# Attention scores taken from float32 q and k directly, in place of rounded halves and remainders

## The chip, the cores and the metric

The kernel runs on one core of a Trainium2 chip. The metric is the device time of one execution in microseconds; the kernel before is given by the median of 3 runs.

## What is computed

Attention with a threshold, 8 batches of 8 heads, 576 queries and keys, 64 columns a head, and behind it an RWKV feed-forward (FFN) on the attention's output. All inputs and the output are float32.

```python
scores = scale * np.matmul(q, k.transpose(0, 1, 3, 2))          # 8 x 8 x 576 x 576
thresh = np.max(scores, axis=-1, keepdims=True) - tau
scores = np.where(scores >= thresh, scores, -1000000000.0)
attn = np.exp(scores - np.max(scores, axis=-1, keepdims=True))
attn = attn / (np.sum(attn, axis=-1, keepdims=True) + 1e-09)
x = np.matmul(attn, v)                       # heads side by side: 8 x 576 x 512
xk = mu_k * x + (1.0 - mu_k) * x_prev        # x_prev: the row before
xr = mu_r * x + (1.0 - mu_r) * x_prev
k = np.maximum(xk @ w_k, 0.0)                # 512 -> 1024
out = sigmoid(xr @ w_r) * (k * k @ w_v)      # 1024 -> 512
```

## The kernel before

The attention goes by jobs: one job is one batch and two heads (32 pairs; batch 0 is cut into two halves, so there are 36 jobs). The two heads' q and k lie transposed in one tile `raw`: 64 rows for each head, 1216 columns (576 of q, 64 last keys, 576 keys). ACT scales the q part by 1/8. A job works in units:

- a P unit is 128 queries of both heads. Its scores fill two PSUM buffers named `s`, one for each head (`s_0`, `s_1`), of 128 x 576 float32 each. There are only these two. There are 128 P units.
- a T unit is the last 64 queries of both heads, in one buffer `s`. There are 32 T units.

For each head of a unit, DVE takes the row maximum (L555), ACT the threshold (L563) and the exponential (L571) from PSUM to `p`, DVE the mask and the row sum (L579), which is the last reader of `s`. DVE inverts the sums (L589, L590), POOL multiplies `p` by them (L604), PE transposes `p` in blocks of 128 (L628) into buffers `w`, ACT and DVE copy them to `pm` and `pl` (L646, L648). Each 256 or 320 queries of a job are one attend (L708): float32 matmuls with 64 weight columns, one head in each half of the array's columns. The result goes to `xT`. Behind each batch stand FFN chunks of 256 rows: L853 for w_k, L895 for w_r, L917 for w_v. The FFN's matmuls take float32r operands, each value as a rounded part and a remainder, three products for each matmul.

The scores use the same idea. ACT rounds `raw` to `hi` (L434), POOL makes the remainder `lo` (L440), and DMAs of the SP queue copy both into `st` tiles of 128 rows: `st1` has hi above lo, `st2` has lo above hi. With 128 rows of contraction, `st1` and `st2` as weights against `st1` as the moving operand give all four products of halves (L521), 4 matmuls of 288 columns for each head. T units use block-diagonal weights `bd` (four ACT copies, L484) and three products (L496). Only the first job (`PLAIN = 1`) takes its scores straight from `raw` in float32 (L510).

Order: every step is given to a planner with an engine, an estimated time and a key; the planner places steps in the order in which they could start, by its own estimates of time and of free buffers. The order of each engine's instructions is then fixed, and an engine goes through its list in order. Scores, transposes and attends have keys far ahead of the FFN's, which fills what is left of PE. In the profile PEld is PE's weight load.

Of the kernel before, what the change touches and what calls it, by code (L numbers as in the profile page):

```python
# [8 lines left out]
F32 = mybir.dt.float32  # L9
FR = mybir.dt.float32r  # L10
AF = mybir.ActivationFunctionType
ALU = mybir.AluOpType
# [205 lines left out]
def tile_threshold_attention_then_rwkv_ffn(  # L218
# [12 lines left out]
    V, A, G, PE, SY = nc.vector, nc.scalar, nc.gpsimd, nc.tensor, nc.sync  # L231
# [3 lines left out]
    P = 128  # L235
    B, NPAIR, _, _ = qk.shape
    D = P // 2
    S = out.shape[1]
# [4 lines left out]
    SM = 512  # L243
    ST = S - SM
    HS = S // 2
    KT = S
    W = 2 * S + ST
# [11 lines left out]
    add = plan.add  # L259
    DQ = 0.55  # L260
    HALF = 1
    W0, W1, W2, W3, AVK = 3.0, 3.5, 50.0, 2.0, 4.5
    PREP, PB, VB, COLD, EARLY = 8, 2, 2, 24, 30
# [3 lines left out]
    def sbuf(tag, shape, dtype=F32, bufs=1):  # L267
        return plan.buf(sb, tag, shape, dtype, bufs)
# [4 lines left out]
    def fixed(name, shape, dtype=F32):  # L273
        return plan.buf(const, name, shape, dtype, make=lambda: const.tile(shape, dtype, name=name))
# [12 lines left out]
        writes=[(small, 0)],  # L287
        key=-100,
# [5 lines left out]
        reads=[(small, 0)],  # L294
        writes=[(small, 1)],
        key=-100,
# [5 lines left out]
        reads=[(small, 0)],  # L302
        writes=[(small, 2)],
        key=-100,
# [8 lines left out]
    xE = fixed("xE", [P, NCT, NE, ST + 1])  # L313


    bd = fixed("bd", [P, 2, P], FR)
    add("DVE", 0.3, lambda: V.memset(bd.get().bitcast(F32), 0.0), writes=[bd], key=-99)

    pieces = {}

    def weight(j, name, w, c, f, key, wait):
# [81 lines left out]
    def operands(job, key):  # L409
        b, hp = job["b"], job["hp"]  # L410
        raw = job["raw"] = sbuf("raw", [P, W], F32, 2)
        add("DMA", DQ, lambda: SY.dma_start(raw.get(), qk[b, hp]), writes=[raw], key=key - PREP - 5, kb=576)
        add(
            "ACT",
            0.67,
            lambda: A.activation(raw.get()[:, 0:S], raw.get()[:, 0:S], AF.Copy, scale=small.get()[:, 2:3]),
            reads=[(small, 2)],
            writes=[raw],
            key=key - PREP,
        )  # L420
        vt = job["v"] = sbuf("v", [P, 5, P], F32, VB)
        add(
            "DMA",
            DQ,
            lambda: SY.dma_start(vt.get(), v[b, hp].rearrange("p (c n) -> p c n", c=5)),
            writes=[vt],
            key=key - 5,
            kb=320,
        )
        if job["plain"]:  # L430

            return
        hi, lo = job["hi"], job["lo"] = sbuf("hi", [P, W], FR), sbuf("lo", [P, W], FR)
        add("ACT", 1.1, lambda: A.activation(hi.get(), raw.get(), AF.Copy), reads=[raw], writes=[hi], key=key - PREP)  # L434
        for y in range(2):
            cs = slice(0, S) if y == 0 else slice(S, W)
            add(
                "POOL",
                1.41 + 0.15 * y,
                lambda cs=cs: G.tensor_tensor(  # L440
                    lo.get()[:, cs], raw.get()[:, cs], hi.get()[:, cs].bitcast(F32), op=ALU.subtract
                ),
                reads=[raw, hi],
                writes=[(lo, y)],
                key=key - PREP,
            )
        job["st"] = [(sbuf("st1", [P, W], FR, 3), sbuf("st2", [P, S], FR, 3)) for _ in range(2)]
        for h in range(2):
            sl = slice(h * D, (h + 1) * D)
            t1, t2 = job["st"][h]  # L450

            up, dn = slice(0, D), slice(D, P)
            for dst, rows, src, n, r in (
                (t1, up, hi, W, (hi, None)),
                (t2, dn, hi, S, (hi, None)),
                (t1, dn, lo, W, (lo, None)),
                (t2, up, lo, S, (lo, 0)),
            ):
                fn = (lambda dst=dst, rows=rows, src=src, n=n, sl=sl: SY.dma_start(
                    dst.get()[rows, 0:n].bitcast(F32), src.get()[sl, 0:n].bitcast(F32)  # L460
                ))
                add("DMA", DQ, fn, reads=[r], writes=[(dst, rows.start)], key=key - PREP, kb=n // 4)

    def scores(unit, ss, key):
        job, c = unit["job"], unit["c"]
        raw = job["raw"]

        def keys(y, z):
            k0 = KT + (ST if unit["kind"] == "P" and y == 0 else 0)
            return slice(k0 + z * HS, k0 + (z + 1) * HS)

        if unit["kind"] == "T" and not job["plain"]:

            hi, lo = job["hi"], job["lo"]
            for v_, src in enumerate((raw, lo)):
                for h in range(2):
                    sl = slice(h * D, (h + 1) * D)  # L480
                    add(
                        "ACT",
                        0.26,
                        lambda v_=v_, src=src, sl=sl: A.activation(  # L484
                            bd.get()[sl, v_, sl], src.get()[sl, SM:S].bitcast(F32), AF.Copy
                        ),
                        reads=[(src, None if v_ == 0 else 0)],
                        writes=[(bd, (v_, h))],
                        key=key - 3,
                    )  # L490
            prods = [(0, hi), (0, lo), (1, hi)]
            for j, (v_, r) in enumerate(prods):

                def mm(j=j, v_=v_, r=r):
                    for z in range(2):
                        PE.matmul(ss[1].get()[:, z, 0:HS], bd.get()[:, v_], r.get()[:, keys(1, z)], start=(j == 0), stop=(j == 2))  # L496

                add("PE", 0.264, mm, reads=[bd, r], writes=[ss[1]], key=key - 1000, lat=0.44)
            return
        if unit["kind"] == "T" or job["plain"]:  # L500

            last = unit["kind"] == "T"

            def both():
                for z in range(2):
                    for h in range(2):
                        hr = slice(h * D, (h + 1) * D)
                        o = ss[1].get()[hr, z, 0:HS] if last else ss[h].get()[:, z, 0:HS]
                        q = slice(SM, S) if last else slice(c * P, (c + 1) * P)
                        PE.matmul(o, raw.get()[hr, q], raw.get()[hr, keys(h, z)], start=True, stop=True)  # L510

            occ = 1.2 if last or key > COLD else 3.0
            add("PE", occ, both, reads=[raw], writes=list(ss.values()), key=key - 1000, lat=occ + 0.25)
            return
        for y in range(2):
            st1, st2 = job["st"][y]
            for j, l in enumerate((st1, st2)):

                def mm(j=j, l=l, r=st1, y=y):
                    for z in range(2):  # L520
                        PE.matmul(  # L521
                            ss[y].get()[:, z, 0:HS],
                            l.get()[:, c * P : (c + 1) * P],
                            r.get()[:, keys(y, z)],
                            start=(j == 0),
                            stop=(j == 1),
                        )

                add("PE", 0.264, mm, reads=[l, st1], writes=[ss[y]], key=key + 0.5 * y - 1000, lat=0.44)

    def softmax(unit):
        n = unit["n"]
# [407 lines left out]


    halved = {j: ([0, 1], [2, "T", 3]) for j in range(HALF)}
    PLAIN = 1
    jobs = []
    n = 0
    for b in range(B):
        for part, order in enumerate(halved.get(b, (["T", 0, 1, 2, 3],))):
            for hp in range(NPAIR):
                job = dict(ji=len(jobs), b=b, hp=hp, first=n, groups={}, plain=len(jobs) < PLAIN, units=[])
                job.update(tail="T" in order, tg=int(part == 1))  # L950
                for u in order:
                    kind = "T" if u == "T" else "P"
                    job["units"].append(dict(job=job, kind=kind, c=u, n=n))
                    n += 1 if kind == "T" else 2
                jobs.append(job)
# [8 lines left out]
    wat = [2.0 + 2.0 * j for j in range(len(wlist))]  # L964

    operands(jobs[0], -1.0)
    add("DMA", DQ, lambda: SY.dma_start(mu_sb.get(), mu.rearrange("p (j c) -> p j c", j=2)), writes=[mu_sb], key=0.0)
    for j, (name, w, c, f) in enumerate(wlist):
        weight(j, name, w, c, f, wat[j], wfr[j])
    for job in jobs:  # L970
        if job["ji"] + 1 < len(jobs):
            operands(jobs[job["ji"] + 1], float(jobs[job["ji"] + 1]["first"]))
        b, seen = job["b"], set()
# [9 lines left out]
        if job["hp"] == NPAIR - 1:  # L983
            key = unit["n"] - 30.0
# [55 lines left out]
```

## Time and profile before

| | |
|---|---|
| median of 3 runs | 1096.16 us (1094.26, 1096.16, 1098.05) |
| span of the profiled execution | 1096.8 us, 0.6 us over that median |
| mean granted clock of TensorE | 0.983 |
| instructions | 19388 |
| DMA | 119.62 MB, 109 GB/s in the mean |
| last scores, last attend | 930 us, 942 us |

The profile comes from one execution, and the time for it is its span. Its page has busy times, a span in 40 slices, the chain of work that ended last, and groups of instructions with the idle time of the engine before them and what ended it ("<-"). Each matmul's end in it is modelled, so start times and steps of the chain say more on PE than busy times do. A float32 matmul of the program stands in the profile as two records; transposes stand as one.

### The profile page before, as it was taken

The numbers are of one execution on the slowest core, as the hardware profiler recorded it, in microseconds if no ns is written. First come the engines' busy times: TensorE is split into PE (matmuls) and PEld (weight loads), VectorE is DVE, ScalarE is ACT, GpSimd is POOL, SyncE is SP. The second block draws the span as 40 slices with busy tenths as digits, with TensorE's granted clock in tenths as the row PEclk, the third lists the DMA queues.
The fourth block names the chain that finished last, engine by engine and source line by source line (L and its number), as shares of the span: only waits on it lengthen the run. The fifth ranks groups of instructions, "written<-read, shape, count | busy, mean of one in ns | idle before, by whom it ended". The sixth has DMA issues, their size and how long they took to land.

```text
span 1096.8 us, 19388 instructions
## 1 busy us (share of the span) xinstructions
PE 1024.5 (93%) x6832; PEld 848.8 (77%) x6832; DVE 769.9 (70%) x1707; ACT 736.4 (67%) x1549; POOL 580.1 (53%) x584
## 2 busy tenths in 40 slices
PE   4667889998999999999999999999999999999998
PEld 3446667776878778788788878886888878888887
DVE  5999978877878788798877858855878488322220
ACT  5766977775876768777678767865777667344442
POOL 4667766544554555456545654654455544344441
PEclk9878999999999999999999999999999999999999
DMA  9994566444444444445444434530645141000000
GB/s 282 227 343 133 138 160 172 118 103 122 103 112 112 103 121 103 113 112 135 105 115 114 108 86 113 122 91 25 143 104 133 36 99 35 20 20 20 20 20 20
DMA packets 41279, 119.62 MB, mean 109 GB/s; under 512 B 6880, under 2 KB 6880, under 8 KB 41184
## 3 DMA queue, kind: packets, MB, share of 16 engines
q1 hardware_dynamic: 41184, 118.39, 41.6%
q8 instruction: 55, 0.90, 0.3%
q14 instruction: 40, 0.33, 0.1%
HBM read 44.70 MB, written 9.44 MB: 49 GB/s over the span
## 4 chain that ended last, share of the span: by engine, by line
PE 72%; DVE 12%; ACT 6%; DMA 5%; POOL 3%; issue 2%; SPq 0%; POOLq 0%; ACTq 0%; DVEq 0%
PE w L853 16%; PE w L917 14%; PE w L708 12%; PE w L628 10%; PE s L521 10%; PE w L895 8%; DMA st<-lo 3%; DVE p L579 3%; DVE mk L810 3%; DVE sm L555 2%; PE s L496 2%; ACT p L571 2%; DMA raw<-in_qk 2%; POOL lo L440 1%; DVE sm L589 1%
## 5 line engine op out<-in xcount | busy, mean ns | idle before, releaser
L604 POOL TENSOR_SCALAR p<-p,sm 128x576 f32<-128x576 f32 x288 | 223.1, 784 | 228.7 <-DVE sm L590 129.4
L579 DVE SCALAR_TENSOR_TENSOR p<-s,sm,p 128x576 f32<-128x576 f32 x288 | 232.8, 813 | 58.6 <-ACT p L571 56.4
L853 PE MATMUL w<-xk,wk 128*128 128x256 f32 x1728 | 237.8, 286 | 1.3 <-POOL xk L831 0.9
L555 DVE TENSOR_REDUCE sm<-s 128x1 f32<-128x576 f32 x288 | 210.8, 750 | 39.7 <-PE s L521 27.6
L853 PEld LDWEIGHTS w<-xk,wk 128*128 128x128 f32 x1728 | 219.4, 190 | 3.8 <-ACT pm L646 1.4
L917 PE MATMUL w<-wv,k 128*128 128x512 f32 x864 | 220.5, 396 | 1.6 <-ACT pm L646 1.5
L628 PE MATMUL w<-ident,p 128*128 128x128 f32 x1312 | 198.2, 283 | 22.6 <-POOL p L604 21.0
L571 ACT ACTIVATE p<-s,sm 128x576 f32<-128x576 f32 x288 | 210.1, 730 | 0.5
L628 PEld LDWEIGHTS w<-ident,p 128*128 128x128 f32 x1312 | 154.3, 144 | 62.0 <-POOL p L604 38.2
L917 PEld LDWEIGHTS w<-wv,k 128*128 128x128 f32 x864 | 155.8, 188 | 30.9 <-ACT pm L646 2.4
L646 ACT ACTIVATE pm<-w 128x512 f32<-128x512 f32 x174 | 102.5, 591 | 81.1 <-PE w L628 80.0
L831 POOL TENSOR_TENSOR xk<-mk,xk 128x512 fp32r<-128x512 f32 x72 | 94.9, 1318 | 104.8 <-ACT xk L823 104.7
L708 PE MATMUL w<-pm,v 128*64 128x256 f32 (+1 forms) x1024 | 144.8, 421 | 3.5 <-DVE pm L648 3.5
L563 ACT ACTIVATE sm<-sm,small 128x1 f32<-128x1 f32 x288 | 83.6, 290 | 93.7 <-DVE sm L555 90.7
L810 DVE SCALAR_TENSOR_TENSOR mk<-m,mu_sb,xT 128x256 f32<-128x256 f32 x128 | 87.2, 721 | 77.1 <-POOL xk L831 77.1
L521 PE MATMUL s<-st 128*128 128x288 f32 x504 | 119.6, 319 | 21.3 <-DVE p L579 15.3
L876 POOL TENSOR_TENSOR k<-r,k 128x512 fp32r<-128x512 f32 x72 | 93.7, 1302 | 71.1 <-ACT k L866 71.0
L440 POOL TENSOR_TENSOR lo<-raw,hi 128x576 fp32r<-128x576 f32 x70 | 105.6, 1526 | 43.6 <-ACT hi L434 36.2
L708 PEld LDWEIGHTS w<-pm,v 128*64 128x64 f32 x1024 | 71.0, 140 | 58.7 <-issue 9.0
L521 PEld LDWEIGHTS s<-st 128*128 128x128 f32 x504 | 82.0, 193 | 40.3 <-issue 25.5
L895 PE MATMUL w<-wr,xk 128*128 128x512 f32 x432 | 110.8, 396 | 1.6 <-ACT pm L646 1.6
L521 PE MATMUL s<-st,st 128*128 128x288 f32 x504 | 111.3, 303 | 0.0
(62 smaller groups left out, 1112.1 us busy)
## 6 DMA issues: line engine op xcount, KB each, us to landing
raw<-in_qk SPq DMA_DIRECT2D x36, 608.0 KB, 5.1
st<-hi SPq DMA_DIRECT2D x70, 304.0 KB, 3.2
st<-lo SPq DMA_DIRECT2D x70, 304.0 KB, 4.2
v<-in_v SPq DMA_DIRECT2D x36, 320.0 KB, 4.3
st<-hi SPq DMA_DIRECT2D x70, 144.0 KB, 3.5
st<-lo SPq DMA_DIRECT2D x70, 144.0 KB, 4.0
out<-sg SPq DMA_DIRECT2D x32, 256.0 KB, 2.0
wk<-in_w_k SPq DMA_DIRECT2D x8, 512.0 KB, 8.8
```

The costliest lines, as they stand in the source:

```text
L440: lambda cs=cs: G.tensor_tensor(lo.get()[:, cs], raw.get()[:, cs], hi.get()[:, cs].bitcast(F32), op=ALU.subtract),
L521: PE.matmul(ss[y].get()[:, z, 0:HS], l.get()[:, c * P : (c + 1) * P], r.get()[:, keys(y, z)], start=(j == 0), stop=(j == 1),)
L555: lambda sv=sv, col=col: V.tensor_reduce(col(0), sv(), axis=AX.XY, op=ALU.max, negate=True),
L571: lambda sv=sv, pv=pv, col=col: A.activation(pv(), sv(), AF.Exp, bias=col(0)),
L579: lambda sv=sv, pv=pv, col=col: V.scalar_tensor_tensor(pv(), sv(), col(1), pv(), op0=ALU.is_ge, op1=ALU.mult, accum_out=col(2)),
L604: lambda y=y: G.tensor_scalar(p.get()[:, y], p.get()[:, y], sm.get()[:, 3, y : y + 1], 0.0, op0=ALU.mult, op1=ALU.add),
L628: PE.transpose(pt.get()[:, c, :], p.get().rearrange("p y s -> p (y s)")[:, o : o + P], ident.get())
L708: PE.matmul(o.get()[hs, 0:n], vt.get()[:, c, hs], pt[:, 0:n], start=(c == 0), stop=(c == 4))
L810: V.scalar_tensor_tensor(d.get()[:, y, o : o + n], diff.get()[:, y, o : o + n], mu_sb.get()[:, j, hc + y : hc + y + 1], prv[:, hc + y], op ...
L853: PE.matmul(h.get()[:, f], l, r, start=(ct == 0 and i == 0), stop=(ct == NCT - 1 and i == 2))
L895: PE.matmul(z.get(), l, r, start=(ct == 0 and i == 0), stop=(ct == NCT - 1 and i == 2))
L917: PE.matmul(vps.get(), l, r, start=(ft == 0 and i == 0), stop=(ft == NFT - 1 and i == 2))
```

## The change

All scores are taken as those of the first job were. The tiles hi, lo, st1, st2 and bd and all their steps go: 35 roundings on ACT, 70 subtractions on POOL, 128 copies on ACT for bd, 280 DMAs. A unit's scores are one step of four float32 matmuls (two halves of the keys, two heads). Head 0 uses rows 0 to 63 of the array, head 1 rows 64 to 127. In a P unit the step writes both buffers `s`; in a T unit head 0 goes to partitions 0 to 63 and head 1 to partitions 64 to 127 of one buffer. The `raw` tile (2 buffers) is now read until the job's last scores.

```diff
-    bd = fixed("bd", [P, 2, P], FR)
-    add("DVE", 0.3, lambda: V.memset(bd.get().bitcast(F32), 0.0), writes=[bd], key=-99)
...
-        if job["plain"]:
-            return
-        hi, lo = job["hi"], job["lo"] = sbuf("hi", [P, W], FR), sbuf("lo", [P, W], FR)
-        add("ACT", 1.1, lambda: A.activation(hi.get(), raw.get(), AF.Copy), reads=[raw], writes=[hi], key=key - PREP)
-        for y in range(2):
...
-        job["st"] = [(sbuf("st1", [P, W], FR, 3), sbuf("st2", [P, S], FR, 3)) for _ in range(2)]
...
-        if unit["kind"] == "T" and not job["plain"]:
...
-            prods = [(0, hi), (0, lo), (1, hi)]
...
-        for y in range(2):
-            st1, st2 = job["st"][y]
-            for j, l in enumerate((st1, st2)):
...
-                add("PE", 0.264, mm, reads=[l, st1], writes=[ss[y]], key=key + 0.5 * y - 1000, lat=0.44)
+        last = unit["kind"] == "T"
+
+        def both():
+            for z in range(2):
+                for h in range(2):
+                    hr = slice(h * D, (h + 1) * D)
+                    o = ss[1].get()[hr, z, 0:HS] if last else ss[h].get()[:, z, 0:HS]
+                    q = slice(SM, S) if last else slice(c * P, (c + 1) * P)
+                    PE.matmul(o, raw.get()[hr, q], raw.get()[hr, keys(h, z)], start=True, stop=True)
+
+        occ = 1.2 if last or key > COLD else 3.0
+        add("PE", occ, both, reads=[raw], writes=list(ss.values()), key=key - 1000, lat=occ + 0.25)
```

The planner then makes a new order. On PE in a late batch, before: one P unit's scores head by head, an attend, transposes, and a T unit's scores. The names' numbers count buffers; `ident` is the unit matrix of the transposes.

```order
L521 MATMUL s_1_7651<-st1_2_6936 128x288 x2
L521 MATMUL s_1_7651<-st1_2_6936,st2_2_6947 128x288 x2
L521 MATMUL s_0_7658<-st1_0_7212 128x288 x2
L521 MATMUL s_0_7658<-st1_0_7212,st2_0_7222 128x288 x2
L708 MATMUL w_2_7668<-pm_1_7549,v_0_7428 64x320 x8
L708 MATMUL w_2_7668<-pl_1_7557,v_0_7428 64x320 x2
L628 MATMUL w_0_7694<-ident_66,p_1_7624 128x128 x4
L628 MATMUL w_1_7700<-ident_66,p_1_7624 128x128 x4
L628 MATMUL w_3_7710<-ident_66,p_1_7624 128x128
L496 MATMUL s_1_7712<-hi_0_7280,bd_79 128x288 x2
L496 MATMUL s_1_7712<-lo_0_7304,bd_79 128x288 x2
L496 MATMUL s_1_7712<-hi_0_7280,bd_79 128x288 x2
```

After, at such a place (scores are L439 now, transposes L541, attends L621, and L830 is w_v):

```order
L830 MATMUL w_0_5365<-wv60_0_936,k2_0_5002 128x512 x3
L621 MATMUL w_3_5436<-pm_0_5295,v_1_4920 64x320 x8
L621 MATMUL w_3_5436<-pl_0_5301,v_1_4920 64x320 x2
L541 MATMUL w_2_5461<-ident_66,p_0_5420 128x128 x4
L541 MATMUL w_1_5467<-ident_66,p_0_5420 128x128 x4
L439 MATMUL s_0_5475<-raw_1_4827 128x288
L439 MATMUL s_1_5477<-raw_1_4827 128x288
L439 MATMUL s_0_5475<-raw_1_4827 128x288
L439 MATMUL s_1_5477<-raw_1_4827 128x288
L541 MATMUL w_3_5482<-ident_66,p_0_5420 128x128
L830 MATMUL w_0_5365<-wv70_0_1020,k2_0_5002 128x512 x3
```

Eight matmuls of 128 rows in two steps have become four of 64 rows that alternate between the two buffers, and the array's mode of use changes ahead of them and behind them.

On DVE, before, around two units of the middle of the kernel (maximum L555, mask L579, a copy L648, the FFN's mix L810):

```order
L555 TENSOR_REDUCE sm_0_6069<-s_0_6107 128x1
L555 TENSOR_REDUCE sm_1_6126<-s_1_6113 128x1
L810 SCALAR_TENSOR_TENSOR mk_0_6140<-m_0_5932,mu_sb_87,xT1_77 128x256 x2
L579 SCALAR_TENSOR_TENSOR p_0_6094,sm_0_6069<-s_0_6107,sm_0_6069,p_0_6094 128x576
L589 TENSOR_SCALAR sm_0_6069<-sm_0_6069 128x2
L590 RECIPROCAL sm_0_6069<-sm_0_6069 128x2
L648 COPY pm_0_6077<-w_1_6150 128x4x128
L579 SCALAR_TENSOR_TENSOR p_1_6166,sm_1_6126<-s_1_6113,sm_1_6126,p_1_6166 128x576
L555 TENSOR_REDUCE sm_1_6126<-s_0_6168 128x1
```

After (maximum L468, mask L492, copy L561):

```order
L468 TENSOR_REDUCE sm_2_4777<-s_0_4762 128x1
L468 TENSOR_REDUCE sm_2_4777<-s_1_4764 128x1
L561 COPY pm_0_4680<-w_0_4780 128x4x128
L492 SCALAR_TENSOR_TENSOR p_0_4789,sm_2_4777<-s_0_4762,sm_2_4777,p_0_4789 128x576
L492 SCALAR_TENSOR_TENSOR p_0_4789,sm_2_4777<-s_1_4764,sm_2_4777,p_0_4789 128x576
L502 TENSOR_SCALAR sm_2_4777<-sm_2_4777 128x2
L503 RECIPROCAL sm_2_4777<-sm_2_4777 128x2
```

Before, the two buffers often belonged to different units (`sm_0` and `sm_1`), and a maximum of the next scores stood right behind one mask. Now both maxima and both masks of one unit stand together.

On PE at the end of batch 1, before (L895 is w_r of the FFN):

```order
L521 MATMUL s_0_2436<-st1_2_2141,st2_2_2153 128x288 x2
L895 MATMUL w_2_2366<-wr10_0_672,xk_1_1410 128x512 x3
L895 MATMUL w_2_2366<-wr20_0_788,xk_1_1410 128x512 x3
L708 MATMUL w_3_2470<-pm_1_2395,v_0_1910 64x256 x8
L708 MATMUL w_3_2470<-pl_1_2420,v_0_1910 64x256 x2
L521 MATMUL s_1_2496<-st1_0_2348 128x288 x2
```

After, in the last units of that batch:

```order
L439 MATMUL s_1_2141<-raw_1_1864 64x288 x4
L541 MATMUL w_0_2153<-ident_66,p_0_2134 128x128 x4
L541 MATMUL w_3_2161<-ident_66,p_0_2134 128x128 x4
L541 MATMUL w_1_2168<-ident_66,p_0_2134 128x128
L439 MATMUL s_0_2172<-raw_1_1864 128x288
L439 MATMUL s_1_2174<-raw_1_1864 128x288
L439 MATMUL s_0_2172<-raw_1_1864 128x288
L439 MATMUL s_1_2174<-raw_1_1864 128x288
L621 MATMUL w_2_2181<-pm_1_2126,v_0_1674 64x256 x8
L621 MATMUL w_2_2181<-pl_1_2132,v_0_1674 64x256 x2
L541 MATMUL w_0_2201<-ident_66,p_1_2159 128x128 x4
```

The FFN's rows that stood between scores here stand further ahead; what is left between one unit's scores and the next are transposes and attends.

More of the change, by code (lines that the diff above doesn't have):

```diff
@@ L429, in operands @@
         )
-        if job["plain"]:
-            return
-        hi, lo = job["hi"], job["lo"] = sbuf("hi", [P, W], FR), sbuf("lo", [P, W], FR)
-        add("ACT", 1.1, lambda: A.activation(hi.get(), raw.get(), AF.Copy), reads=[raw], writes=[hi], key=key - PREP)
-        for y in range(2):
[L436 to L446, printed above, removed]
-        job["st"] = [(sbuf("st1", [P, W], FR, 3), sbuf("st2", [P, S], FR, 3)) for _ in range(2)]
[L448 to L462, printed above, removed]
     def scores(unit, ss, key):
@@ L473, in keys @@
             return slice(k0 + z * HS, k0 + (z + 1) * HS)
-        if unit["kind"] == "T" and not job["plain"]:
-            hi, lo = job["hi"], job["lo"]
-            for v_, src in enumerate((raw, lo)):
+        last = unit["kind"] == "T"
+        def both():
+            for z in range(2):
                 for h in range(2):
[L480 to L490, printed above, removed]
-            prods = [(0, hi), (0, lo), (1, hi)]
[L492 to L514, printed above, removed]
@@ L515, in scores @@
-        for y in range(2):
-            st1, st2 = job["st"][y]
-            for j, l in enumerate((st1, st2)):
[L519 to L527, printed above, removed]
-                add("PE", 0.264, mm, reads=[l, st1], writes=[ss[y]], key=key + 0.5 * y - 1000, lat=0.44)
+                    hr = slice(h * D, (h + 1) * D)
@@ L942, in tile_threshold_attention_then_rwkv_ffn @@
     halved = {j: ([0, 1], [2, "T", 3]) for j in range(HALF)}
-    PLAIN = 1
     jobs = []
@@ L948, in tile_threshold_attention_then_rwkv_ffn @@
             for hp in range(NPAIR):
-                job = dict(ji=len(jobs), b=b, hp=hp, first=n, groups={}, plain=len(jobs) < PLAIN, units=[])
+                job = dict(ji=len(jobs), b=b, hp=hp, first=n, groups={}, units=[])
                 job.update(tail="T" in order, tg=int(part == 1))
```

## The prediction

> **What bounds the kernel now.** I read the page's busy line and its chain of work that ended last first, then the busy times by stretch of the span, because the kernel has a ramp, a long mixed stage and a tail. Columns after the window: its length, then busy time of PE, PEld, DVE, ACT and POOL, the granted clock of TensorE, DMA share and GB/s.
>
> ```profile
> PE 1024.5 (93%) x6832; PEld 848.8 (77%) x6832; DVE 769.9 (70%) x1707; ACT 736.4 (67%) x1549; POOL 580.1 (53%) x584
> ...
> PE 72%; DVE 12%; ACT 6%; DMA 5%; POOL 3%; issue 2%; SPq 0%; POOLq 0%; ACTq 0%; DVEq 0%
> ```
>
> ```profile
> 0.00:27.00 27.00, 11.50 (x42) 8.47 (x42) 14.56 (x31) 14.70 (x26) 11.20 (x15) 1.00 0.90 280
> 27.00:150.00 123.00, 91.22 (x530) 68.88 (x530) 114.20 (x208) 90.94 (x187) 83.03 (x67) 0.88 0.72 201
> 150.00:470.00 320.00, 306.15 (x2114) 249.60 (x2112) 257.53 (x580) 234.24 (x521) 175.23 (x183) 0.99 0.48 121
> 470.00:942.00 472.00, 465.51 (x3263) 388.21 (x3261) 352.32 (x818) 337.04 (x724) 252.11 (x267) 1.00 0.39 96
> 942.00:1097.00 155.00, 150.14 (x890) 133.66 (x888) 31.27 (x73) 59.52 (x95) 58.56 (x54) 1.00 0.06 21
> ```
>
> From 150 us to the last attend at 942 us PE (TensorE) idles 20 us of 792 (306.15 and 465.51 busy), and the FFN tail behind it is PE as well. Only the ramp up to 150 us has another limit: there DVE is busy 114 of 123 us. So after 150 us a microsecond of PE work more or less is a microsecond of time, and what leaves ACT, POOL and the DMA engines counts only where PE waited for it. The chain that ended last says the same: 72% of it is PE.
>
> **The change, part by part.** The price of PE work stands in the chain in order of time (start, length, what; lengths are steps of the chain, so no overlap):
>
> ```profile
> 501.98 2.31 PE w L708 x20
> 504.29 0.69 PE w L628 x5
> 504.99 1.06 PE s L521 x8
> ...
> 510.97 0.98 PE w L628 x9
> ...
> 518.13 0.55 PE w L628 x5
> ...
> 520.51 2.84 PE w L708 x20
> 523.35 0.70 PE w L628 x5
> 524.04 0.80 PE s L496 x6
> ```
>
> *Removed on PE.* Scores of a pair of heads and 128 queries (a P unit) are the 8 matmuls of 1.06 us; the 64 last queries of both heads (a T unit) the 6 matmuls of 0.80 us.
>
> *Added on PE: streaming.* The only row-tiled float32 matmuls of before are those of the first job (L510), in the ramp:
>
> ```profile
> 8.15 2.29 PE L510 MATMUL s<-raw 64*128 64x288 f32 x8 [8.15 <-ACT raw L416]
> ...
> 16.20 2.18 PE L628 MATMUL w<-ident,p 128*128 128x128 f32 x9
> 22.97 0.82 PE L521 MATMUL s<-st 128*128 128x288 f32 x2 [4.59 <-DMA st<-lo]
> ```
>
> Eight records for the four matmuls of one P unit: a float32 matmul runs as two. Nine transposes took 2.18 us here and 0.98 at 511 us, so PE ran 2.2 times slower in this place. The 2.29 us are then 1.03 at the later speed, first weights and end included; that is a lower end for a P unit. The heads do share the time. The attends (L708) give the rate at full speed: they are float32 too, two heads at a time, in the column halves. Ten pairs cost 2.31 us at 256 columns and 2.84 at 320, so 0.53/640 = 0.83 ns a column, and a pair of 288 columns 0.24 us. A unit's four pairs stream 0.96 us.
>
> *Added on PE: entering and leaving a tiled mode.* Of the attend's 2.31 us, 10 x 256 x 0.83 ns = 2.12 are streaming, 0.19 are left. The five transposes behind it took 0.69 and 0.70 us where others took 0.55: 0.14 more. So a visit to the column mode costs about 0.33 us. No row shows the row mode at full speed. I take 0.33 for it, from the nearest rows; its ends are 0.07 (the 1.03 above less 0.96) and 0.40 (its weights are 128 columns wide, those of the attends 64).
>
> *Sum on PE.* A unit costs 0.96 + 0.33 = 1.29 us. P: 126 units x (1.29 - 1.06) = +29.0 (128 units less the two of the first job, which were so already). T: 32 x (1.29 - 0.80) = +15.7. In the new order of PE full, row-tiled and column-tiled stretches meet 425 times, before 131 times; 294 more boundaries are 147 visits, not 158, since some units stand beside attends: -11 x 0.33 = -3.6. Together +41 us. The FFN, the transposes and the attends stay as they are; about 50 us of FFN move from behind the last attend to ahead of it, which changes no sum.
>
> How much of it is on the path: scores by stretch, counted by the row maximum of each head (L555):
>
> ```profile
> 0.00:150.00 150.00, 24.23 (x33) 0.90 0.75 215
> 150.00:470.00 320.00, 80.77 (x110) 0.99 0.48 121
> 470.00:942.00 472.00, 105.81 (x145) 1.00 0.39 96
> ```
>
> 255 of 288 heads lie where PE is the limit: 41 x 0.885 = **+36 us**. The rest lies beside DVE's work of the ramp; without that cover it would be the other 5.
>
> *Removed elsewhere* (a group of the page, three groups with their shapes kept apart, then the list of waits):
>
> ```profile
> L440 POOL TENSOR_TENSOR lo<-raw,hi 128x576 fp32r<-128x576 f32 x70 | 105.6, 1526 | 43.6 <-ACT hi L434 36.2
> ```
>
> ```profile
> L434 ACT ACTIVATE hi<-raw 128x1216 fp32r<-128x1216 f32 x35 | 42.6, 1218 | 10.3 <-PE s L496 9.0 <-DMA st<-lo 1.1
> ...
> L484 ACT ACTIVATE bd<-lo 64x64 fp32r<-64x64 f32 x64 | 16.2, 253 | 2.2 <-POOL lo L440 1.3
> L484 ACT ACTIVATE bd<-raw 64x64 fp32r<-64x64 f32 x64 | 16.1, 251 | 1.2 <-PE s L496 0.7
> ```
>
> ```profile
> PE w L628 <- POOL p L604: 21.0, 20, 4.5
> PE s L521 <- DVE p L579: 15.3, 13, 2.6
> ...
> PE s L521 <- DMA st<-lo: 5.3, 2, 4.6
> ```
>
> ACT loses 42.6 + 16.2 + 16.1 = 75 us, POOL 105.6, the SP queue 280 copies. Neither engine bounds. What it can give is PE's waits (the last fence: total us, times, longest). The wait for a copy of lo goes: the second job's scores at 23 us waited 4.59 for it, **-4**. Its next limit is the ACT step that scales raw, which stays. Transposes waited 21.0 us for POOL's normalization p. POOL's queue gets shorter by 105.6 of 580 us, so a share goes; between 0 and 21 I take **-8**, since the same POOL instructions wait mostly for DVE. The copies themselves land while PE works and are worth nothing more; their cover is PE, which stays full.
>
> *Added: a wait.* One PE step now writes both score buffers, s_0 and s_1, so it stands until the masks (L579) of both heads before it have released them; behind it in PE's queue stand transposes and FFN matmuls. Before, each head's scores waited for one buffer, and DVE masked one head while PE filled the other. The new cycle of a P unit, from these rows:
>
> ```profile
> L579 DVE SCALAR_TENSOR_TENSOR p<-s,sm,p 128x576 f32<-128x576 f32 x288 | 232.8, 813 | 58.6 <-ACT p L571 56.4 <-PE s L521 0.3
> ...
> L555 DVE TENSOR_REDUCE sm<-s 128x1 f32<-128x576 f32 x288 | 210.8, 750 | 39.7 <-PE s L521 27.6 <-PE s L510 6.6 <-PE s L496 3.0
> L571 ACT ACTIVATE p<-s,sm 128x576 f32<-128x576 f32 x288 | 210.1, 730 | 0.5
> ...
> L563 ACT ACTIVATE sm<-sm,small 128x1 f32<-128x1 f32 x288 | 83.6, 290 | 93.7 <-DVE sm L555 90.7 <-DVE sm L589 1.8
> ...
> L579 DVE DVE_READ_ACCUMULATOR p<-s,sm,p 128x1 f32 x288 | 23.6, 82 | 0.0
> ```
>
> Scores 1.29, first maximum 0.75, threshold and exponential 0.29 + 0.73, two masks of 0.81 + 0.08: 4.85 us. A T unit has one mask: 3.95. Where PE has less than that to do from one unit to the next, it idles. The new order shows where: in the last eight units of batch 1 no FFN matmul stands at all (before, some 16 us of FFN stood there), only 1.29 + 9 transposes of 0.98 and some attends; four of those units have about 2.3 us of work, and the eight together fall 12 us short. The ends of batches 2 and 3 fall 4 us short each. **+20** for all, with 0 and 35 as ends (none if FFN or POOL lag anyway; more if ACT's and DVE's queues delay each hand-over).
>
> *Sum:* 1096.8 (the profiled span, 0.6 over the median of 1096.16) + 36 - 4 - 8 + 20 = 1140.8. **Forecast 1140 us.** For that case alone the ends give 1112 (row visits at 0.14, no new idle time) to 1162.
>
> **Rivals.** (a) *Faster: the row mode costs nothing to enter.* Then P units change by 0.96 - 1.06 and T units by 0.96 - 0.80: -12.6 + 5.1 = -7.5 us, and with the 4 of the ramp about 1085. It decides below 0.05 us a visit (7.5 over 147). For it: the 1.03 us above. Against it: 0.33 in every attend. In the Trainium skill, "TensorE: Matmul & The Clock Gate", section "Measured speedup vs the span model", packed tiles take one matmul's time plus about 4 ns a tile, with no charge for changing the mode; by that the sum is this rival's. The attend rows speak against it. Chance 0.06.
>
> (b) *The two heads of a T unit run one after the other,* because both write one bank of PSUM. 32 x 0.96 = 31 us more: 1171. Against it: the two heads of an attend share a bank in the column mode and share the time. For it: in a P unit the heads have different buffers, so no row shows two row halves in one bank. The Trainium skill, "TensorEngine Tiling (Array Packing)", "Gotcha 1: PSUM Pressure", says that different row tiles cannot access one bank at the same time; no run here shows that yet. Chance 0.12.
>
> (c) *The cycle becomes the bound.* 128 x 4.85 + 32 x 3.95 = 747 us, against some 915 between 27 and 942; with 1.3 us of queueing in each unit it exceeds that and PE idles all through. Half of it idle: 30 us more, 1170. PE's idle time in the windows before 470 us might also lower the clock, as in the window with 0.88. For it: PE waited 15.3 us for masks already. Chance 0.15.
>
> (d) *Most is hidden:* PE's 20 us of idle time after 150 us take up the extra work, and the relief of POOL is whole: 1096.8 + 36 - 20 - 4 = 1109, or down to no change. Chance 0.08.
>
> **How the numbers follow.** The forecast has 0.59 and the rivals 0.06, 0.12, 0.15 and 0.08. This measurement can tell about 0.3% (3.3 us) from no change. Faster: (a), and a hundredth of (d), 0.07. Same: 0.04, of (d). Slower: the rest, 0.89. The range leaves out (a) and a part of (d) below, and the upper parts of (b) and (c): 1104 to 1176, likeliest 1140.
>
> **What would show it.** In the profile after: a P unit of about 1.29 us and a T unit likewise in the chain (1.9 us or more for T would be rival (b)); transposes behind scores 0.14 us longer; PE's sum up with about the same idle time; ACT near 660 and POOL near 475 us busy; at the end of batch 1 PE waits for DVE's mask; the last attend later, near 1030 us, and a tail near 105. The prediction is wrong if row visits are cheap, or if PE's waits for POOL were what held the middle stage.

## The result, and the profile after

The change makes the kernel slower: 1155.74 us in the median (1152.98 to 1156.84, 4 runs) against 1095.38, a ratio of 1.0539 with an interval of 1.0518 to 1.0561. The profiled executions have spans of 1155.1 and 1096.8 us, so 58.3 us are to be explained. The forecast was 1140, its range 1104 to 1176.

The page after: its busy line and the chain of work that ended last.

```profile
PE 1087.2 (94%) x6896; PEld 796.6 (69%) x6896; DVE 765.6 (66%) x1706; ACT 670.4 (58%) x1390; POOL 480.0 (42%) x514
...
PE 79%; DVE 9%; ACT 6%; POOL 3%; issue 3%; DMA 0%; POOLq 0%; SPq 0%; DVEq 0%; ACTq 0%
```

Busy times by stretch (window, its length, PE, PEld, DVE, ACT, POOL, clock of TensorE, DMA share, GB/s), first of the kernel after, then of the kernel before:

```profile
0.00:150.00 150.00, 110.11 (x561) 68.29 (x562) 123.56 (x242) 92.26 (x190) 76.47 (x72) 0.87 0.36 127
150.00:942.00 792.00, 769.49 (x5032) 560.54 (x5031) 545.81 (x1248) 474.27 (x1006) 321.03 (x358) 0.99 0.12 39
942.00:1155.00 213.00, 207.61 (x1310) 167.81 (x1306) 96.19 (x218) 103.88 (x196) 82.46 (x85) 1.00 0.08 25
```

```profile
0.00:150.00 150.00, 102.72 (x571) 77.35 (x572) 128.76 (x238) 105.64 (x212) 94.22 (x81) 0.90 0.75 215
150.00:942.00 792.00, 771.66 (x5375) 637.80 (x5373) 609.85 (x1397) 571.28 (x1244) 427.34 (x450) 1.00 0.43 106
```

ACT lost 66 us and POOL 100, and PE gained 63. Between 150 and 942 us PE idles 22.5 us (before 20.3), though it gets through fewer matmuls. So at first sight the time went into PE's work. The chain after shows the prices (the names of lines: L439 scores, L541 transposes, L621 attends, L766 and L808 FFN):

```profile
565.43 0.58 PE w L541 x4
566.02 1.17 PE s L439 x8
567.19 0.70 PE w L541 x5
567.88 0.36 PE w L766 x3
568.24 2.73 PE w L808 x12
570.97 1.12 PE s L439 x8
572.09 2.27 PE w L808 x9
```

The first group of L439 is a P unit, the second a T unit; the timeline tells them apart by their shapes, 64*128 and 64*64. A P unit costs 1.17 us and 0.15 in the transposes behind it (0.70 where 0.55 is usual): 1.32, where the kernel before paid 1.06. A T unit costs 1.12 and, with the same 0.15 behind it, 1.27, before 0.80. (The nine matmuls of L808 behind this one take 0.22 more than at the rate of the twelve before it, so its 0.15 is rather low.)

The profile after also has something that busy times do not show. At the end of batch 1, PE's own rows of the timeline (start, length, in brackets the idle time before and what ended it):

```profile
260.11 1.49 PE L541 MATMUL w<-ident,p 128*128 128x128 f32 x9
263.22 0.72 PE L439 MATMUL s<-raw 64*128 64x288 f32 x2 [1.62 <-DVE p L492]
264.20 1.74 PE L439 MATMUL s<-raw 64*128 64x288 f32 x6 [0.26 <-DVE p L492]
265.86 2.18 PE L541 MATMUL w<-ident,p 128*128 128x128 f32 x9
...
275.92 1.19 PE L439 MATMUL s<-raw 64*64 64x288 f32 x8 [2.09 <-issue]
278.39 2.18 PE L541 MATMUL w<-ident,p 128*128 128x128 f32 x9 [1.29 <-POOL p L517]
```

PE waits for DVE's mask (L492), as forecast for this place, and then nine transposes take 2.18 us, what they took in the slow ramp of the kernel before: the clock of TensorE fell (granted between 264 and 268 us: 0.59). For the 2.09 us ahead of the T unit at 275.92 the profile names no releaser. The mean clock is 0.975 after and 0.983 before. In the clock records of the two traces, 52.5 us of PE's busy time lie in stretches of half clock after and 31.7 before. At half clock half of that time is lost, so an estimate of 10 us more is lost to the clock. The mean clock alone says less: other executions of the kernel before show 0.975 with a span of 1092.9 us and 0.986 with 1095.2.

### The profile page after: what moved, and what is told of

It is laid out like the page before. It is cut to its first block, busy times and chain, and to the rows that moved or that the text cites. A ratio compares the mean times of both kernels' runs of the same rounds, so it can differ in the third digit from the quotient of the medians.

```text
span 1155.1 us, 18576 instructions
## 1 busy us (share of the span) xinstructions
PE 1087.2 (94%) x6896; PEld 796.6 (69%) x6896; DVE 765.6 (66%) x1706; ACT 670.4 (58%) x1390; POOL 480.0 (42%) x514
## 4 chain that ended last, share of the span: by engine, by line
PE 79%; DVE 9%; ACT 6%; POOL 3%; issue 3%; DMA 0%; POOLq 0%; SPq 0%; DVEq 0%; ACTq 0%
PE w L766 18%; PE w L830 14%; PE s L439 14%; PE w L541 12%; PE w L621 12%; PE w L808 9%; DVE p L492 3%; POOL p L517 2%; ACT p L484 2%; DVE sm L502 1%; ACT L484 1%; DVE sm L468 1%; ACT pm L559 1%; DVE mk L723 1%; DVE xT L371 1%
## 5 line engine op out<-in xcount | busy, mean ns | idle before, releaser
L517 POOL TENSOR_SCALAR p<-p,sm 128x576 f32<-128x576 f32 x288 | 231.6, 813 | 392.6 <-DVE sm L503 375.5
L468 DVE TENSOR_REDUCE sm<-s 128x1 f32<-128x576 f32 x288 | 206.8, 751 | 119.6 <-PE s L439 119.0
L492 DVE SCALAR_TENSOR_TENSOR p<-s,sm,p 128x576 f32<-128x576 f32 x288 | 233.2, 815 | 75.5 <-ACT p L484 75.0
L439 PE MATMUL s<-raw 64*128 64x288 f32 (+1 forms) x1280 | 215.2, 440 | 36.2 <-issue 17.9
L766 PE MATMUL w<-xk,wk 128*128 128x256 f32 x1728 | 240.5, 291 | 4.2 <-ACT xk L736 3.2
L766 PEld LDWEIGHTS w<-xk,wk 128*128 128x128 f32 x1728 | 218.2, 192 | 20.1 <-issue 11.5
L830 PE MATMUL w<-wv,k 128*128 128x512 f32 x864 | 223.0, 402 | 0.0
L541 PE MATMUL w<-ident,p 128*128 128x128 f32 x1312 | 202.6, 289 | 20.1 <-POOL p L517 18.2
L541 PEld LDWEIGHTS w<-ident,p 128*128 128x128 f32 x1312 | 152.9, 146 | 88.5 <-POOL p L517 53.7
L439 PEld LDWEIGHTS s<-raw 64*128 64x128 f32 (+1 forms) x1280 | 112.9, 182 | 104.3 <-issue 65.9
L830 PEld LDWEIGHTS w<-wv,k 128*128 128x128 f32 x864 | 155.4, 188 | 41.3 <-issue 10.9
L621 PE MATMUL w<-pm,v 128*64 128x256 f32 (+1 forms) x1024 | 152.7, 425 | 2.8 <-ACT pm L559 2.4
L744 POOL TENSOR_TENSOR xk<-mk,xk 128x512 fp32r<-128x512 f32 x72 | 92.2, 1281 | 144.1 <-ACT xk L736 137.9
L621 PEld LDWEIGHTS w<-pm,v 128*64 128x64 f32 x1024 | 71.1, 140 | 68.0 <-issue 14.1
L723 DVE SCALAR_TENSOR_TENSOR mk<-m,mu_sb,xT 128x256 f32<-128x256 f32 x128 | 81.3, 675 | 46.0 <-POOL xk L744 45.0
L808 PE MATMUL w<-wr,xk 128*128 128x512 f32 x432 | 110.9, 399 | 0.0
L561 DVE COPY pm<-w 128x512 f32<-128x512 f32 x114 | 78.4, 688 | 37.5 <-PE w L541 37.3
L808 PEld LDWEIGHTS w<-wr,xk 128*128 128x128 f32 x432 | 77.4, 188 | 18.7 <-issue 3.1
```

The source lines that it names most:

```text
L468: lambda sv=sv, col=col: V.tensor_reduce(col(0), sv(), axis=AX.XY, op=ALU.max, negate=True),
L492: lambda sv=sv, pv=pv, col=col: V.scalar_tensor_tensor(pv(), sv(), col(1), pv(), op0=ALU.is_ge, op1=ALU.mult, accum_out=col(2)),
L517: lambda y=y: G.tensor_scalar(p.get()[:, y], p.get()[:, y], sm.get()[:, 3, y : y + 1], 0.0, op0=ALU.mult, op1=ALU.add),
L541: PE.transpose(pt.get()[:, c, :], p.get().rearrange("p y s -> p (y s)")[:, o : o + P], ident.get())
L621: PE.matmul(o.get()[hs, 0:n], vt.get()[:, c, hs], pt[:, 0:n], start=(c == 0), stop=(c == 4))
L766: PE.matmul(h.get()[:, f], l, r, start=(ct == 0 and i == 0), stop=(ct == NCT - 1 and i == 2))
```

## The experiments

All ratios are against the kernel before, 1095.8 to 1097.1 us in these runs.

**1. The wait for both buffers alone.** The kernel before with a P unit's eight matmuls in one step, where the kernel before has four steps of two:

```diff
-                add("PE", 0.264, mm, reads=[l, st1], writes=[ss[y]], key=key + 0.5 * y - 1000, lat=0.44)
+        add("PE", 1.056, joint, reads=[t for y in range(2) for t in job["st"][y]],
+            writes=list(ss.values()), key=key - 1000, lat=1.232)
```

> The kernel before with one thing of the change: the eight matmuls of a P unit's scores (still rounded halves, full array) are one step that writes both score buffers, so a unit waits for both. Theory 'modes' (the +58 us of the span are PE work: entering and leaving the row mode, and streaming): PE's work is unchanged, so 1095 to 1101 us. Theory 'lock step' (a third or more of the +58 comes from waiting for both buffers, as the prediction's +20 has it): 1112 us or more.

1151.33 us, 1.0501 (1.0483 to 1.0518). Nearly the whole +58 without a single row-tiled matmul more. Its busy line and its busy times by stretch, and PE's waits between 150 and 942 us there (total us, times, longest) and then in the kernel before:

```profile
PE 1049.2 (91%) x6832; PEld 864.6 (75%) x6832; DVE 787.8 (69%) x1707; ACT 743.5 (65%) x1553; POOL 582.9 (51%) x584
...
0.00:150.00 150.00, 91.68 (x491) 69.46 (x492) 121.27 (x212) 94.76 (x187) 87.08 (x75) 0.81 0.72 199
150.00:942.00 792.00, 757.74 (x5074) 625.05 (x5072) 572.18 (x1284) 544.02 (x1166) 409.72 (x423) 0.97 0.41 102
```

```profile
PE s L496 <- DVE p L578: 12.0, 9, 2.2
PE w L627 <- POOL p L603: 11.5, 22, 1.0
PE s L520 <- DVE p L578: 7.6, 6, 3.6
```

```profile
PE w L628 <- POOL p L604: 4.9, 6, 1.2
PE s L521 <- DVE p L579: 4.6, 6, 1.9
```

Waits of scores for masks grew from some 5 to 19.6 us. PE's idle time grew by 28 us (span less busy time, 100.3 against 72.3): 11 up to 150 us, 14 from there to 942, the rest behind. And the same 6832 matmuls keep PE busy 24.7 us longer. Together that is the 52.7 by which the spans differ (1149.5 and 1096.8). The mean clock fell to 0.955, and 74.0 us of PE's busy time lie at half clock where 31.7 did: by the same estimate 21 of the 24.7. About two fifths of the price of the wait is then not waiting but the lower clock that comes with it. The joint step also makes the planner place the steps in another order; the wait in the old order was not measured.

**2. Visits to the row mode alone.** The kernel before, its order unchanged, with one small row-tiled matmul behind each unit's scores (behind the T units' in the same way):

```diff
+                    if y == 1 and j == 1:
+                        PE.matmul(ss[1].get()[:, 1, HS : HS + 16], ident.get()[0:D, :],
+                                  ident.get()[0:D, 0:16], start=True, stop=True)
```

> The kernel before, its order unchanged, with a small row-tiled float32 matmul (64 rows, 16 columns, into unused columns of the score buffer) behind each unit's scores: the visits to the row mode alone, without the wait for both buffers. Two theories now, since joint scores alone cost +55 us. 'Either alone': the visits (158 x 0.3 to 0.45 us, nine tenths on the path) cost 1095 + 43 to 64 without the wait as well, so 1138 to 1160 us, and in the kernel after the two overlap: PE's extra work fills the time that the wait opens. 'Wait only': visits hide beside other work, under 1115 us, and the whole +58 is the wait.

1157.44 us, 1.0559 (1.0535 to 1.0583): +61.5, or 0.39 us for each of 158 visits, the small matmul included. The array changes its mode 426 times in this run, in the kernel after 425 times. In its chain the small matmul stands between the scores and what follows (L523 scores, L531 the small matmul, a float32 matmul being two records):

```profile
505.64 0.52 PE s L523 x4
506.16 0.32 PE s L531 x2
...
509.49 0.54 PE s L523 x4
510.03 0.36 PE w L857 x3
510.39 0.53 PE s L523 x4
510.92 0.32 PE s L531 x2
511.25 1.26 PE w L857 x9
```

It takes 0.32 us for 16 columns, and the matmuls behind it a little longer (1.26 for nine where three take 0.36). In these lines nothing of it is hidden; over the whole run PE is busy 74.1 us longer (1098.6) and the span grows by 61.4. Visits cost time without the wait too, and "wait only" falls. How much of the 0.39 is the small matmul and how much the visit, the next run tells.

**3. A second visit in each unit.** The kernel after with a small matmul of the whole array between the second and third matmul of a unit, and as a control the same matmul behind the fourth:

```diff
                     PE.matmul(o, raw.get()[hr, q], raw.get()[hr, keys(h, z)], start=True, stop=True)
+                if z == 0:
+                    PE.matmul(ss[1].get()[:, 1, HS : HS + 16], ident.get(), ident.get()[:, 0:16], start=True, stop=True)
```

> The kernel after with a small matmul of the whole array (16 columns, into unused columns of the score buffer) between the second and the third matmul of each unit's scores, so that each unit enters the row mode twice. 'Modes': 160 further visits of 0.3 to 0.4 us, nine tenths of them on the path, and the small matmuls: 1156 + 45 to 75, so 1200 to 1230 us, and 40 to 60 us above the control. 'Lock step': PE time in a unit is partly hidden beside the wait for the buffers, under 25 us above the control.

> The control of the run with split visits: the kernel after with the same small matmul behind the fourth matmul of each unit, so no further visit to the row mode. Both theories: only the small matmul itself, 160 x 0.05 to 0.15 us, 1160 to 1180 us.

1226.23 us (1.1193, 1.1173 to 1.1213) and 1186.99 (1.0824, 1.0796 to 1.0852). The control's +31 is dearer than the 4 to 24 expected: 0.2 us a unit, though its small matmul adds no visit. In its chain (L440 is the small matmul, L542 transposes):

```profile
511.75 1.17 PE s L439 x8
512.93 0.32 PE s L440 x2
513.25 0.59 PE w L542 x5
```

The small matmul takes 0.32 us, as in run 2, and the transposes behind it 0.59 where 0.70 stands behind a unit in the kernel after. The split is 39 above the control, 0.25 us for each of 160 further visits, just below the 40 to 60 expected. PE is busy 39.0 us longer there than in the control (1163.9 and 1124.9), so its work is on the path in the kernel after too. All three kernels of this comparison (after, split, control) have the same order on PE. At the control's price the small matmuls are some 30 of run 2's 61.5 us, which leaves some 30 for the visits: by this estimate the visits alone do not cost what the whole change costs.

**4. The T units alone.** The kernel before without `bd`; T units from `raw`:

```diff
-        if unit["kind"] == "T" and not job["plain"]:
...
-                add("PE", 0.264, mm, reads=[bd, r], writes=[ss[1]], key=key - 1000, lat=0.44)
```

> The kernel before with only the T units taken from float32 q and k in the two halves of the array's rows (no block-diagonal tile; the P units keep their halves). 'Modes': each T unit costs 1.12 us from its first matmul to the next step's, 0.10 to enter and 0.06 to 0.12 behind it, against 0.80: 32 x 0.5 = +16, so 1107 to 1113 us. A rival by which the 64 ACT copies saved are worth something: under 1100 us.

1118.73 us, 1.0208 (1.0190 to 1.0226): +23, above the expected +16. In the profiled execution PE is busy 16.5 us longer than before (1041.0 and 1024.5), near 32 x 0.47 = 15 by the T unit's price, and the span is 18.6 longer; where the rest comes from is not shown. No gain shows from the 64 copies on ACT for each of raw and lo, which are gone here.

**5. The P units alone.** P units from `raw`, T units as before; hi and lo are still made, the copies to `st` are gone:

```diff
-        job["st"] = [(sbuf("st1", [P, W], FR, 3), sbuf("st2", [P, S], FR, 3)) for _ in range(2)]
...
-        if unit["kind"] == "T" or job["plain"]:
+        if True:
```

> The kernel before with only the P units taken from float32 q and k (both buffers in one step); T units keep hi, lo and the block-diagonal tile, the copies st1 and st2 are gone. 'Modes': 126 x (1.17 + 0.10 + 0.09 - 1.06) = +38, nine tenths of it on the path, and a few us of lower clock: 1130 to 1142 us; with the T units' part the sum of both is the whole +60. 'Lock step': also near there, but then the run with joint scores alone shows a third or more of it.

1151.76 us, 1.0495 (1.0465 to 1.0525), above the expected 1142. With the T units' +23 the two parts sum to +78, not to +60: the parts do not add up, but each of these runs still carries rounding that the change removes, and each has an order of its own.

**6. The relief undone.** The kernel after with hi, lo and their copies to `st` put back, unused (the 128 copies for `bd` stay out):

```diff
+        hi, lo = job["hi"], job["lo"] = sbuf("hi", [P, W], FR), sbuf("lo", [P, W], FR)
+        add("ACT", 1.1, lambda: A.activation(hi.get(), raw.get(), AF.Copy), reads=[raw], writes=[hi], key=key - PREP)
...
+                add("DMA", DQ, fn, reads=[r], writes=[(dst, rows.start)], key=key - PREP, kb=n // 4)
```

> The kernel after with the roundings, subtractions and copies of before put back, their results unused: 35 x 1.2 us on ACT, 70 x 1.5 us on POOL, 280 DMAs; the scores stay as after. It undoes the relief of the other engines alone. If the relief is worth what the prediction took (8 + 4 us): 1164 to 1170 us. If it is worth nothing, since PE bounds: 1153 to 1160 us. If the relief hides a larger loss: over 1175 us.

1175.13 us, 1.0704 (1.0674 to 1.0734), which is 1.65% of 1095 or 18 us above the kernel after and above the 1164 to 1170 by the prediction's price. So work that left ACT, POOL and the DMAs was worth up to 18 us, though PE is the busiest engine by far; the planner makes another order here too, and what that alone does is not separated. A likely reason, not shown by itself: in the kernel after a unit's cycle (scores, maxima, exponentials, masks, scores) runs through DVE and ACT, and what stands in their queues lengthens it. The busy times of this run have the clock at 0.78 up to 150 us and PE idle 28 us from there to 942:

```profile
0.00:150.00 150.00, 104.22 (x493) 64.22 (x493) 124.55 (x227) 91.14 (x181) 91.72 (x79) 0.78 0.72 211
150.00:942.00 792.00, 764.02 (x4980) 560.69 (x4980) 544.18 (x1220) 501.71 (x1017) 391.34 (x404) 0.99 0.38 96
```

**7. The order.** Four runs change only the planner's numbers, or a step's size, to see how much of the price the order makes. First the kernel after with the scores' estimate as measured:

```diff
-        occ = 1.2 if last or key > COLD else 3.0
+        occ = 1.38 if last or key > COLD else 3.0
```

> The kernel after with the planner's estimate for a unit's scores at 1.38 us in place of 1.2 (the visit as measured), so a new order. 'Modes': the work is the same and PE's waits are as before, 1150 to 1162 us. A rival by which the order, made with a wrong cost, costs the time: under 1145 us.

1148.91 us, 1.0470 (1.0438 to 1.0501): a gain of about 7 us, between the two expected ranges. Then all the softmax estimates as measured, in the kernel after and in the kernel before:

```diff
-                0.67,
+                0.75,
                 lambda sv=sv, col=col: V.tensor_reduce(col(0), sv(), axis=AX.XY, op=ALU.max, negate=True),
...
-                0.74,
+                0.9,
                 lambda sv=sv, pv=pv, col=col: V.scalar_tensor_tensor(
```

> The kernel after with the planner's estimates of the softmax steps set to what the trace shows (maximum 0.75, threshold 0.29, exponential 0.73, mask 0.90, inversion 0.46, normalization 0.80, copies 0.59 and 0.69, scores 1.38 us), so a new order. If the wait for both buffers costs what it does because the planner places a unit's scores on PE before the masks are done: 1125 to 1145 us. If PE's work sets the time: 1146 to 1158 us.

> The kernel before with the same estimates (its scores' estimate unchanged): the control of the run with new costs, and a candidate. If the estimates matter only where a unit waits for both buffers: 1092 to 1102 us.

1196.91 us (1.0910, 1.0885 to 1.0934) and 1105.74 (1.0088, 1.0070 to 1.0107). Truer estimates made both orders worse, against what I expected; the kernel with the joint step loses 41 us by it, the other 10. Last, the joint scores of run 1 with softmax estimates at 0.65, so that the attention is planned earlier and the FFN kept for later:

> The kernel before with joint scores, as in the run with joint scores alone, and the planner's estimates of the softmax steps (maximum, threshold, exponential, mask, inversion, normalization) at 0.65 of what they were, so that it plans the attention earlier: 140 us of FFN behind the last attend in place of 98 (149 in the kernel before). PE's work is that of before. If the +55 us of joint scores come from the order (FFN spent early, nothing left to fill the waits): 1096 to 1125 us. If they come from the wait for both buffers itself, whatever the order: 1135 us or more.

1207.51 us, 1.1012 (1.0984 to 1.1041). So FFN spent too early does not explain the price of run 1; planned earlier, PE stands in front of the two buffers and of POOL's p all the time:

```profile
PE w L627 <- POOL p L603: 59.9, 98, 4.0
PE s L520 <- DVE p L578: 20.4, 15, 8.9
PE s L496 <- DVE p L578: 12.3, 12, 2.6
```

Both directions being worse, these runs show that the kernels with joint scores are far more sensitive to the order (7 to 56 us here), not what the best order would give. Runs 1, 4, 5 and 6 have new orders as well, so their sizes hold only with that reserve; runs 2 and 3 do not.

**8. Fewer visits in the kernel before.** Both attends of a job as one step:

```diff
+                    if len(job["units"]) < 5:
+                        attend(job, g, unit["n"] + (AVK if unit["n"] < 20 else 1.5))
+                    elif g == 1:
+                        attend_both(job, unit["n"] + 1.5)
```

> The kernel before with the two attends of a job made one step (20 pairs in one visit to the column mode): 81 boundaries of modes in place of 131, so 25 visits fewer. 'Modes': 25 x 0.33 = -8 us, 1085 to 1091 us, if holding the transposed tiles longer adds no wait. If a visit cost little, or the longer step delays scores: 1094 us or more.

1101.50 us, 1.0044 (1.0028 to 1.0059): not faster, 5 us slower. The waits of P units' scores for masks over the whole span rose from 15.3 to 20.9 us (the list of waits of this run):

```profile
PE w L628 <- POOL p L604: 22.7, 24, 4.5
PE s L521 <- DVE p L579: 20.9, 23, 2.6
```

A step of 5 us on PE holds up the scores behind it; that this is the whole of the missing 13 us is not shown. No version here beats the kernel before.

## Why the prediction was right, and where its sum was not

The direction and the range held, and each price of PE's work too; two of the terms beside it, the wait and the relief, were too small.

- *A unit's 1.29 us.* Right: 1.32 for P and 1.27 for T in the chain after. Less 0.96 of streaming, the visit in the row mode costs 0.31 to 0.36 us, about what the attends' visit in the column mode costs (0.33), and 0.25 in run 3; rival (a), by which it is free to enter, falls with run 3. The Trainium skill's span model ("TensorE: Matmul & The Clock Gate", "Measured speedup vs the span model") holds for the pairs, whose two heads start 7 ns apart here, but not for the change of mode, which it leaves out: 0.25 us a visit in run 3.
- *T units in one bank.* Rival (b) falls: the T unit's 8 records take 1.12 us, less than a P unit's, so the heads share the time. The Trainium skill's rule on row tiles in one bank ("TensorEngine Tiling (Array Packing)", "Gotcha 1: PSUM Pressure") does not show here, where the two row halves write different partitions.
- *Nine tenths of PE's work on the path.* About right: of PE's added busy time 0.83 reaches the span in run 2, 0.78 in run 3's control (29.5 of 37.7 us) and all of it between control and split. Rival (d) falls.
- *The first wait for a copy, -4.* Right in kind: the second job's scores start at 19.46 us, before at 22.97.

```profile
19.46 1.29 PE L439 MATMUL s<-raw 64*128 64x288 f32 x2 [1.57 <-issue]
```

- *The relief of ACT and POOL, -8 with the -4 beside it.* Mis-sized: run 6 gives up to 18 us for both, its order included.
- *The wait for both buffers, +20.* Mis-sized, and the worst step. I counted PE's idle time where no FFN stands, and left the clock to a rival. Alone, with the order that comes with it, the wait costs 55 us (run 1): 28 of idle time and 25 in which the same matmuls take longer, most of that the clock.
- *The sum.* I added the terms. The runs speak against that. One path through them: before to joint scores +55 (run 1), float32 and row mode with the halves still made +22 (1.0704 less 1.0501, run 6) where the unit prices below give 44 us of PE work, the relief -18, together +59. The reading is that PE's added work fills the time in which it would wait: between 150 and 942 us it idles 34.3 us with the wait alone and 22.5 with both. How large the overlap is stays open, since these runs differ in order as well. That the forecast of +44 came within 16 us of the measured +60 was in part luck: a wait taken too small and an overlap left out stood against each other.
- *The ends for the forecast's own case.* The low one, 1112, does not come out of its terms: row visits at 0.14 make 147 x 0.14 - 7.5 = 13 us of PE work, 12 of it on the path, and without new idle time the sum is 1096.8 + 12 - 4 - 8 = 1097, no change. The high one, with visits at 0.40, comes to 1165.
- *Rival (c),* the cycle as the bound: its mechanism shows in run 1, though not as idle time in the kernel after. It had a chance of 0.15 where it deserved to be part of the sum.
- The last attend starts at 1051.6 us, forecast near 1030; ACT is busy 670 (660), POOL 480 (475).

Not settled: about 8 us. In the two profiled executions PE is busy 62.7 us longer and idle 4.4 us less, which is the whole 58.3. Of the 62.7 the unit prices give 126 x 0.26 + 32 x 0.47 = 48 us, less 3.6 for shared boundaries, and the clock 10 by the estimate above. That is 54 of 62.7.

## What to carry to other kernels

Before a row- or column-tiled step replaces full-array work, count how often the array changes its mode, not only the columns it streams: here 0.25 to 0.36 us for each visit, against 0.96 us of streaming. A step that takes all the buffers of a loop at once couples engines that ran apart; its price is the idle time and then the clock that falls with it, and it shows even where PE looks 91% busy (run 1). Parts that overlap cannot be summed: run each alone, then together, and hold the order of the engines where you can, since a new order alone was worth 7 to 56 us here.

## What was not expected of the hardware

- The clock fell with short gaps: in the kernel after, gaps of 1 to 2 us between bursts at the end of a batch came with nine transposes of 2.18 us, more than twice the 0.98 of the full clock. With joint scores alone the mean clock was 0.955, at PE 91% busy.
- In the traces of the kernels before and after, of run 1 and of its early order in run 7, the clock changes on a grid of 3.41 us. Leaving out the first 7 and the last 4 us, each of the 42 changes to half clock follows a grid step in which PE was busy 0.56 of the time or less, 40 of them one under 0.5. Only four steps under 0.5 at full clock were not followed by half clock. So a gap of 2.1 us and one of 1.3 within 5 us, as at 276 us in the kernel after, were enough.
- A float32 matmul of 16 columns took 0.32 us of the chain, a third of a whole unit's streaming, in the row mode (run 2) and with the whole array (run 3) alike.
